# Three mantissa bits of float64 weights taken by ScalarE, and one VectorE operation for each attention tile's bias and threshold

## Chip, cores and metric

The kernel runs on one core of one Trainium2 chip. The metric is the device time of one execution in microseconds. The engines are PE (TensorE, with PEld for its weight loads), DVE (VectorE), ACT (ScalarE), POOL (GpSimd) and SP (SyncE, which here issues nearly all transfers).

## What is computed

Three layers in a row on 2304 tokens of width 512. The second layer's weights arrive as float64.

```python
scores = scale * np.matmul(q, k.transpose(0, 1, 3, 2))        # 4 batches, 8 heads, 576 x 576, depth 64
thresh = np.max(scores, axis=-1, keepdims=True) - tau
scores = np.where(scores >= thresh, scores, -1000000000.0)
scores = scores - np.max(scores, axis=-1, keepdims=True)
attn = np.exp(scores)
attn = attn / (np.sum(attn, axis=-1, keepdims=True) + 1e-09)
x = np.matmul(attn, v)                                        # then heads side by side: 2304 x 512
...
xn = x / rms * rms_g
g = xn @ w_gate                                               # 512 x 1536
x = (g * sigmoid(g) * (xn @ w_val)) @ w_out                   # 1536 x 512
...
P = 8 rounds of row and column scaling of exp(x @ w_gate)     # 8 experts
out += P[:, e:e + 1] * (np.maximum(x @ w1[e], 0.0) @ w2[e])   # for each expert e
```

## The kernel before

**Number format.** Matrices are split into a high and a low f16 part, and a product is three f16 matmuls. The float64 weights of the second layer are read as pairs of 32-bit words. `to_f32` makes a float32 of each: ACT turns the upper word, read as a float, into the right exponent (L441, `wo<-wgatew`, the name `wo` is the staging place). DVE shifts the lower word right by 29, which leaves its top three bits (L442, into `lw`, shown as `wgatel`, `wvall` or `wol`). DVE shifts the float left by three and ORs those bits in (L444). DVE puts the sign in (L445). Each such piece is 128 rows of 512 weights. There are 36: 12 of `w_gate`, 12 of `w_val`, 12 of `w_out`. ACT then squares each piece (L465 for gate and val, whose column sums PE takes; L499 for `w_out`), scales come from that, and L474 and L475 write the high and low parts of `wg` and `wv`. L516 to L518 write those of `wo` when all 12 pieces of `w_out` are done, a maximum over all partitions (`womx`) is known, and the scale is made.

**Attention.** There are 144 tiles of 128 query rows by 576 keys: 36 in each batch, one for each head and block of rows (`att_tile`). PE makes the scores `S` (L282) in one of two PSUM buffers. DVE takes the maximum of each row (L296, into column 2 of the small tile `nt`). ACT multiplies it with a factor `wt` to give the bias of the exponential (L297, column 0), and adds `bt` to it to give the threshold (L301, column 1). ACT makes `e = exp(c2 * S + bias)` (L300), and DVE zeroes what lies under the threshold, and sums the rows (L302). Only L302 frees the buffer of `S`. ACT and POOL then split `e` into `hl` (L307 to L309), SP turns it by a DMA transpose into `eT` (L319), and four tiles later PE multiplies it with `v` (L339, `pv`).

**Order of the work.** Attention of batch 0 runs beside the preparation of the weights. When 16 tiles have gone through `end_main` and `finish_x` (L355 to L362), the second layer starts on PE: `mlp_in` (12 groups `gv` of 24 matmuls, L539, emptied by ACT L547 and DVE L548 and L549) and `mlp_out` (72 matmuls, L573). From there on attention tiles and the second layer share all engines until about 620 us. The third layer (L1020 and L1088) follows to the end. A scheduler works out the order on each engine from dependences and a cost of each instruction, with attention ahead of all else, so a changed instruction can reorder its neighbours. Each engine then executes its list strictly in that order.

Of the kernel before, what the change touches and what calls it, by code (L numbers as in the profile page):

```python
# [8 lines left out]
F16 = mybir.dt.float16  # L9
BF16 = mybir.dt.bfloat16  # L10
I32 = mybir.dt.int32
AF = mybir.ActivationFunctionType
ALU = mybir.AluOpType
AX = mybir.AxisListType
# [5 lines left out]
def kernel(  # L20
# [29 lines left out]
    P = 128  # L50
# [6 lines left out]
    NW = NCH + 1  # L57
# [3 lines left out]
    def small(shape, name, dt=F32, bufs=1):  # L61
        return p0.tile(shape, dt, tag=name, name=name, bufs=bufs)
# [130 lines left out]
    def prep_q_scales(st):  # L193

        b, qr = st["b"], st["raw_q"]
        s_k, i_k = st["k"]
        qm = small([P, NW], "qm", bufs=2)
        for c in range(NW):
            sq = pa.tile([P, H, 2, D], F16, tag="ks", name=f"qq{b}_{c}", bufs=2)
            A.activation(  # L200
                sq[:, :, 0, :].bitcast(BF16), qr[:, :, c, :], AF.Square, accum_out=qm[:, c : c + 1]
            )
        s_q, i_q = norm_scale(qm, NW, 9, f"q{b}")

        wt = small([P, NW], f"wt_{b}")
        bt = small([P, NW], f"bt_{b}")
        V.tensor_scalar(bt, s_q, s_k[:, 0:1], ntau8[:, 0:1], ALU.mult, ALU.mult)
        c2 = small([P, NW], f"c2_{b}")
        V.tensor_scalar(c2, i_q, i_k[:, 0:1], z8[:, 0:1], ALU.mult, ALU.mult)
        V.tensor_scalar(wt, i_q, i_k[:, 0:1], nz8[:, 0:1], ALU.mult, ALU.mult)  # L210
        st.update(wt=wt, bt=bt, c2=c2, s_q=s_q)

    def prep_k(st, a):
# [57 lines left out]
    def att_tile(st, c, heads, slot, group):  # L271

        kT = st["kT"]
        qT, qX = st["q", c]
        nm = f"{st['b']}_{c}_{heads[0]}"
        sums = group["sums"]
        sp = psa.tile([P, 2, 512], F32, tag="S", name=f"S{nm}", bufs=2)
        rows = P // len(heads)
        for qq, first in ((qT, True), (qX, False)):
            for i, h in enumerate(heads):  # L280
                for j in range(2):
                    last = T.matmul(  # L282
                        sp[i * rows : (i + 1) * rows, j, 0:HS],
                        lhsT=qq[:, h, 0:rows],
                        rhs=kT[h // H2][:, h % H2, j * HS : (j + 1) * HS],
                        start=first,
                        stop=not first,
                    )
        if len(waiting) == LAG:
            with tc.issue_after(last.ins):  # L290
                att_values(*waiting.pop(0))
        turn()
        sv = sp[:, :, 0:HS]
        nt = pa.tile([P, 3], F32, tag="nt", name=f"nt{nm}", bufs=4)
        mx = nt[:, 2:3]
        V.tensor_reduce(mx, sv, AX.XY, ALU.max)  # L296
        A.activation(nt[:, 0:1], mx, AF.Copy, scale=st["wt"][:, c : c + 1])  # L297
        e = pa.tile([P, S], F32, tag="e", name=f"e{nm}", bufs=3)
        ev = e.rearrange("p (a n) -> p a n", a=2)
        A.activation(ev, sv, AF.Exp, bias=nt[:, 0:1], scale=st["c2"][:, c : c + 1])  # L300
        A.activation(nt[:, 1:2], mx, AF.Identity, bias=st["bt"][:, c : c + 1])  # L301
        V.scalar_tensor_tensor(  # L302
            ev, sv, nt[:, 1:2], ev, ALU.is_ge, ALU.mult, accum_out=sums[:, slot : slot + 1]
        )

        hl = pa.tile([P, 2 * S], F16, tag="hl", name=f"hl{nm}", bufs=3)
        A.activation(hl[:, 0:S], e, AF.Copy)  # L307
        G.tensor_tensor(hl[:, S + REM :], e[:, 0 : NCH * P], hl[:, 0 : NCH * P], ALU.subtract)  # L308
        G.tensor_tensor(hl[:, S : S + REM], e[:, NCH * P :], hl[:, NCH * P : S], ALU.subtract)  # L309
        waiting.append((st, heads, slot, group, nm))  # L310
        split[nm] = hl
# [110 lines left out]
    def words(src, name, tag="tT"):  # L422

        if tag == "tT":
            r = pw.tile([P, 4, 2, 2 * P], F16, tag=tag, name=name, bufs=4)
            r = r.rearrange("p f l n -> p (f l n)").bitcast(I32)
        else:
            r = pw.tile([P, 4, HD], F32, tag=tag, name=name)
            r = r.rearrange("p o d -> p (o d)").bitcast(I32)
        nc.sync.dma_start(out=r, in_=src)  # L430
        return r.rearrange("p (n w) -> p n w", w=2)

    def to_f32(dst, word, name):

        lw = pw.tile([P, 2, 2, HD], F16, tag="xs", name=name, bufs=2)
        lw = lw.rearrange("p o l n -> p (o l n)").bitcast(I32)  # L440
        A.activation(dst, word[:, :, 1].bitcast(F32), AF.Copy, scale=2.0**-112)  # L441
        V.tensor_scalar(lw, word[:, :, 0], 29, None, ALU.logical_shift_right)  # L442
        di = dst.bitcast(I32)
        V.scalar_tensor_tensor(lw, di, 3, lw, ALU.logical_shift_left, ALU.bitwise_or)  # L444
        V.scalar_tensor_tensor(  # L445
            di, word[:, :, 1], -(2**31), lw, ALU.bitwise_and, ALU.bitwise_or
        )
        return lw
# [785 lines left out]
```

## Time and profile before

| | us |
|---|---|
| median of 3 runs (all: 2121.09, 2122.43, 2131.33) | 2122.43 |
| profiled execution | 2124.11 |
| its span between first and last instruction | 2122.3 |
| PE busy (share of the span) | 1951.8 (92%) |
| DVE busy | 1628.7 (77%) |
| ACT busy | 1307.6 (62%) |
| POOL busy | 1357.4 (64%) |

The profile cuts the span into 40 slices of 53 us. PE is busy for one to four tenths of the first three, and for eight or nine tenths of nearly all others. DVE is at nine tenths in the second and third slice. A busy time is the union of an engine's instructions. An instruction's duration is longer than the time until the next one may start (its step), because neighbours overlap a little. So costs of an engine that has no pause are read as the distance of two starts.

### The profile page before, as it was taken

The page shows a single profiled execution, that of the slowest core. Times are in us where ns is not written, and L with a number is a line of the kernel's source. Part 1 is how long each engine was busy: PE and PEld are TensorE (multiplying, and loading weights), DVE is VectorE, ACT ScalarE, POOL GpSimd, SP SyncE. Part 2 cuts the span into 40 slices and gives each one's busy share as a digit, 9 for nine tenths or more (in the row PEclk, how much of TensorE's full clock was granted, in tenths as well). Part 3 has the DMA queues.
Part 4 walks back from the last instruction along what each step waited for, and adds up shares of the span by engine and source line. Part 5 has one row for each costly group of instructions (what it writes and reads, how often), then busy time and mean ns, then how long its engine had stood idle before and what let it go on. Part 6 is the DMA issues. An engine that isn't in the chain of part 4 may idle for free.

```text
span 2122.3 us, 43825 instructions
## 1 busy us (share of the span) xinstructions
PE 1951.8 (92%) x16462; PEld 1453.5 (68%) x16462; DVE 1628.7 (77%) x3408; ACT 1307.6 (62%) x2804; POOL 1357.4 (64%) x1412
## 2 busy tenths in 40 slices
PE   1348889998999899899999999999999999999998
PEld 0227667667777667677777777777777777777777
DVE  6999777777753445897888888888888878888865
ACT  6888787877753356556655555565555555555552
POOL 0347556656753456667777767777677777777754
PEclk9959999999999999999999999999999999999999
DMA  9986778878756736333433443444334334443332
GB/s 260 224 191 126 158 145 163 169 132 142 134 96 147 186 104 183 123 109 121 140 121 122 125 144 118 124 124 135 120 114 142 118 124 121 141 125 120 102 100 80
DMA packets 373094, 290.47 MB, mean 137 GB/s; under 512 B 286160, under 2 KB 299344, under 8 KB 372880
## 3 DMA queue, kind: packets, MB, share of 16 engines
q1 hardware_dynamic: 371712, 285.81, 52.3%
q8 instruction: 129, 2.11, 0.4%
q0 software_dynamic: 640, 1.84, 0.3%
q14 instruction: 85, 0.70, 0.1%
q10 hardware_dynamic: 528, 0.02, 0.0%
HBM read 195.71 MB, written 21.23 MB: 102 GB/s over the span
## 4 chain that ended last, share of the span: by engine, by line
PE 67%; DVE 2%; SPq 1%; DMA 1%; POOL 1%; ACT 0%; issue 0%; DVEq 0%; POOLq 0%; ACTq 0%
PE P L1088 31%; PE X L1020 17%; PE Z L1020 13%; PE gv L539 3%; PE x L573 2%; SPq L831 1%; DVE w L731 1%; DMA w1r<-in_moe_w_dram 0%; DMA xo<-x2d 0%; DMA eT<-hl 0%; DVE acc L1102 0%; PE logits L873 0%; PE pv L339 0%; DVE w1mx L133 0%; DVE h L999 0%
## 5 line engine op out<-in xcount | busy, mean ns | idle before, releaser
L1088 PE MATMUL P<-w,h 128*128 128x256 f16 x6048 | 769.8, 273 | 12.3 <-DVE w1mx L133 7.6
L1088 PEld LDWEIGHTS <-h 128*128 128x128 f16 x6048 | 592.4, 98 | 151.6 <-issue 15.6
L1020 PEld LDWEIGHTS <-w 128*128 128x128 f16 x4032 | 394.8, 98 | 194.1 <-issue 2.9
L1098 DVE SCALAR_TENSOR_TENSOR acc<-P,coef,acc 128x256 f32<-128x256 f32 x882 | 413.2, 477 | 101.3 <-PE P L1088 90.4
L1020 PE MATMUL X<-xo,w 128*128 128x384 f16 x2304 | 437.9, 327 | 1.3 <-ACT u2b L1040 0.9
L1020 PE MATMUL Z<-xo,w 128*128 128x384 f16 x1728 | 327.9, 326 | 0.0
L308 POOL TENSOR_TENSOR hl<-e,hl 128x512 f16<-128x512 f32 x144 | 174.1, 1209 | 226.9 <-ACT hl L307 148.1
L539 PE MATMUL gv<-xnT,wg 128*128 128x256 f16 x1296 | 170.5, 282 | 17.4 <-DVE u L549 11.9
L539 PE MATMUL gv<-xnT,wv 128*128 128x256 f16 x1296 | 168.5, 276 | 0.0
L539 PEld LDWEIGHTS <-wg 128*128 128x128 f16 x1296 | 128.3, 101 | 38.6 <-issue 18.4
L573 PE MATMUL x<-wo,tT 128*128 128x512 f16 x648 | 143.8, 379 | 3.8 <-DVE u L549 2.5
L539 PEld LDWEIGHTS <-wv 128*128 128x128 f16 x1296 | 126.4, 99 | 16.6 <-issue 0.2
L302 DVE SCALAR_TENSOR_TENSOR e<-S,nt,e 128x576 f32<-128x576 f32 x144 | 116.6, 810 | 24.8 <-ACT e L300 24.4
L296 DVE TENSOR_REDUCE nt<-S 128x1 f32<-128x576 f32 x144 | 107.0, 750 | 26.7 <-PE S L282 25.9
L300 ACT ACTIVATE e<-S,nt,c 128x576 f32<-128x576 f32 x144 | 117.8, 818 | 0.0
L282 PE MATMUL S<-kT,qT 128*128 128x288 f16 (+1 forms) x320 | 65.2, 311 | 56.4 <-DVE e L302 52.1
L573 PEld LDWEIGHTS <-tT 128*128 128x128 f16 x648 | 62.4, 98 | 75.2 <-ACT wo L517 2.7
L339 PEld LDWEIGHTS <-eT 128*128 128x128 f16 (+1 forms) x2240 | 89.1, 106 | 33.4 <-DMA eT<-hl 18.5
L307 ACT ACTIVATE hl<-e 128x576 f16<-128x576 f32 x144 | 97.0, 675 | 23.9 <-DVE e L302 14.8
L339 PE MATMUL pv<-vs,eT 128*128 128x64 f16 (+1 forms) x2240 | 97.4, 201 | 14.8 <-DMA eT<-hl 12.5
L554 POOL TENSOR_TENSOR tT<-u,tT 128x256 f16<-128x256 f32 x108 | 75.4, 699 | 54.7 <-ACT tT L553 54.3
L548 DVE SCALAR_TENSOR_TENSOR u<-u,gv 128x256 f32<-128x256 f32 x108 | 44.8, 415 | 63.7 <-ACT u L547 61.8
(2540 smaller groups left out, 3675.8 us busy)
## 6 DMA issues: line engine op xcount, KB each, us to landing
xo<-x2s SPq DMA_DIRECT2D x319, 384.0 KB, 3.1
w1r<-in_moe_w_dram SPq DMA_DIRECT2D x17, 1024.0 KB, 5.1
w2r<-in_moe_w_dram SPq DMA_DIRECT2D x17, 1024.0 KB, 6.7
x2s<-xo SPq DMA_DIRECT2D x17, 384.0 KB, 3.6
wgatew<-in_moe_w_gate_dram SPq DMA_DIRECT2D x12, 512.0 KB, 6.0
wo<-in_moe_w_out_dram SPq DMA_DIRECT2D x12, 512.0 KB, 4.3
wvalw<-in_moe_w_val_dram SPq DMA_DIRECT2D x12, 512.0 KB, 4.5
qX<-qT SPq DMA_DIRECT2D x40, 128.0 KB, 2.7
```

What stands on the lines that cost most here:

```text
L296: V.tensor_reduce(mx, sv, AX.XY, ALU.max)
L300: A.activation(ev, sv, AF.Exp, bias=nt[:, 0:1], scale=st["c2"][:, c : c + 1])
L302: V.scalar_tensor_tensor(ev, sv, nt[:, 1:2], ev, ALU.is_ge, ALU.mult, accum_out=sums[:, slot : slot + 1])
L307: A.activation(hl[:, 0:S], e, AF.Copy)
L308: G.tensor_tensor(hl[:, S + REM :], e[:, 0 : NCH * P], hl[:, 0 : NCH * P], ALU.subtract)
L339: T.matmul(o, lhsT=a, rhs=r, start=n == 0, stop=n == len(mm) - 1)
L539: T.matmul(gv[:, a, :], lhsT=w[:, l, kk, f * P : (f + 1) * P], rhs=xt[:, r * KD + kk, :], start=n == 0, stop=n == 3 * KD - 1,)
L554: G.tensor_tensor(t[:, 1, :], u, t[:, 0, :], ALU.subtract)
L573: T.matmul(ps, lhsT=tT[f][:, l, o : o + P], rhs=wo[:, f, r, :], start=n == 0, stop=n == 3 * KF - 1,)
L1020: T.matmul(ps, lhsT=w[:, a, l, kk, f * P : (f + 1) * P], rhs=xb[:, r * 2 + kk, :], start=n == 0 and j in (0, 1, 3), stop=n == 5, skip_grou ...
L1088: T.matmul(ps, lhsT=hs[u, ao, f][:, l, jj * P : (jj + 1) * P], rhs=w2[h][:, bo, r, f, :], start=n == 0 and j in (0, 1, 3), stop=n == 5, sk ...
L1098: main[True] = V.scalar_tensor_tensor(y, ps, coef[h][:, i : i + 1], y, ALU.mult, ALU.add)
```

## The change

Two edits. In `to_f32` the shift on DVE is gone. ACT reads the upper 16 bits of the lower word as an unsigned integer, multiplies by 2^-13, subtracts a half (but for 2^-15) and writes an integer, whose rounding gives the top three bits. In `att_tile` the two ACT operations are gone. `wt` and `bt` become pairs, (factor, 1) and (0, offset), and one DVE operation makes both columns of `nt` from the row maximum. The pairs take two buffers in turn for four batches, and each batch adds two small memsets.

```diff
-        wt = small([P, NW], f"wt_{b}")
-        bt = small([P, NW], f"bt_{b}")
-        V.tensor_scalar(bt, s_q, s_k[:, 0:1], ntau8[:, 0:1], ALU.mult, ALU.mult)
+        wt = small([P, NW, 2], "wt", bufs=2)
+        bt = small([P, NW, 2], "bt", bufs=2)
+        V.memset(wt[:, :, 1], 1.0)
+        V.memset(bt[:, :, 0], 0.0)
+        V.tensor_scalar(bt[:, :, 1], s_q, s_k[:, 0:1], ntau8[:, 0:1], ALU.mult, ALU.mult)
...
-        V.tensor_scalar(wt, i_q, i_k[:, 0:1], nz8[:, 0:1], ALU.mult, ALU.mult)
+        V.tensor_scalar(wt[:, :, 0], i_q, i_k[:, 0:1], nz8[:, 0:1], ALU.mult, ALU.mult)
...
-        A.activation(nt[:, 0:1], mx, AF.Copy, scale=st["wt"][:, c : c + 1])
+        V.scalar_tensor_tensor(nt[:, 0:2], st["wt"][:, c], mx, st["bt"][:, c], ALU.mult, ALU.add)
         e = pa.tile([P, S], F32, tag="e", name=f"e{nm}", bufs=3)
         ev = e.rearrange("p (a n) -> p a n", a=2)
         A.activation(ev, sv, AF.Exp, bias=nt[:, 0:1], scale=st["c2"][:, c : c + 1])
-        A.activation(nt[:, 1:2], mx, AF.Identity, bias=st["bt"][:, c : c + 1])
...
-        return r.rearrange("p (n w) -> p n w", w=2)
+        return r.rearrange("p (n w) -> p n w", w=2), r.bitcast(U16).rearrange("p (n w) -> p n w", w=4)
...
-    def to_f32(dst, word, name):
+    def to_f32(dst, words, name):
+        word, half = words
...
-        V.tensor_scalar(lw, word[:, :, 0], 29, None, ALU.logical_shift_right)
+        A.activation(lw, half[:, :, 1], AF.Copy, scale=2.0**-13, bias=2.0**-15 - 0.5)
```

The lines after the edits move down by four at most. In the changed kernel the conversion is L445 (upper word) and L446 (new) on ACT and L448 and L449 on DVE. The attention tile is L299 (maximum), L300 (new, on DVE), L303 (exponential) and L304 (threshold and sum).

On ACT, at the first pieces of `w_gate`, before:

```order
L441 ACTIVATE wo<-wgatew_0_877 128x512
L441 ACTIVATE wo<-wgatew_1_887 128x512
L255 ACTIVATE qs_0_160<-raw_q_112,q_s 128x8x64
L224 ACTIVATE ks_0_0_169<-raw_k_104,k_s 128x4x64 x2
L465 ACTIVATE wgateq_0_884<-wo 128x512
```

Now:

```order
L445 ACTIVATE wo<-wgatew_0_859 128x512
L446 ACTIVATE wgatel_0_861<-wgatew_0_859 128x512
L258 ACTIVATE qs_0_162<-raw_q_112,q_s 128x8x64
L227 ACTIVATE ks_0_0_171<-raw_k_104,k_s 128x4x64 x2
L445 ACTIVATE wo<-wgatew_1_869 128x512
L446 ACTIVATE wgatel_1_871<-wgatew_1_869 128x512
```

ACT now has two whole-piece operations for every piece ahead of DVE's two.

On DVE, where the first group of the second layer (`gv_0`) is emptied (`u_0`), before:

```order
L445 SCALAR_TENSOR_TENSOR wo<-wo_1709,wol_1711 128x512
L296 TENSOR_REDUCE nt_3_1_2115<-S_3_1_2094 128x1
L302 SCALAR_TENSOR_TENSOR e_3_0_2066,sums_3_2041<-S_3_0_2042,nt_3_0_2063,e_3_0_2066 128x576
L501 TENSOR_TENSOR om<-om,igv 128x12
L548 SCALAR_TENSOR_TENSOR u_0_1270<-u_0_1270,gv_0_1245 128x256
L501 TENSOR_TENSOR om<-om,igv 128x12
L549 SCALAR_TENSOR_TENSOR u_0_1270<-u_0_1270,gv_0_1245 128x256
```

Now:

```order
L449 SCALAR_TENSOR_TENSOR wo<-wo_1651,wol_1653 128x512
L552 SCALAR_TENSOR_TENSOR u_0_1252<-u_0_1252,gv_0_1227 128x256
L304 SCALAR_TENSOR_TENSOR e_3_0_2044,sums_3_2019<-S_3_0_2020,nt_3_0_2041,e_3_0_2044 128x576
L299 TENSOR_REDUCE nt_3_1_2092<-S_3_1_2071 128x1
L553 SCALAR_TENSOR_TENSOR u_0_1252<-u_0_1252,gv_0_1227 128x256
L300 SCALAR_TENSOR_TENSOR nt_3_1_2092<-wt,nt_3_1_2092,bt 128x2
L299 TENSOR_REDUCE nt_3_2_2135<-S_3_2_2114 128x1
L552 SCALAR_TENSOR_TENSOR u_1_1284<-u_1_1284,gv_1_1259 128x256
L300 SCALAR_TENSOR_TENSOR nt_3_2_2135<-wt,nt_3_2_2135,bt 128x2
L304 SCALAR_TENSOR_TENSOR e_3_1_2095,sums_3_2019<-S_3_1_2071,nt_3_1_2092,e_3_1_2095 128x576
L553 SCALAR_TENSOR_TENSOR u_1_1284<-u_1_1284,gv_1_1259 128x256
L448 SCALAR_TENSOR_TENSOR wol_1661<-wo,wol_1661 128x512
```

Before, the last of the 36 pieces is done ahead of `u_0` (L501 takes the maxima of `w_out` right behind it). Now 31 are done there, and five pieces of `w_out` stand among the groups of the second layer.

On DVE, two tiles of batch 1 (blocks 2, heads 0 and 1), before:

```order
L296 TENSOR_REDUCE nt_2_0_3756<-S_2_0_3735 128x1
L302 SCALAR_TENSOR_TENSOR e_1_7_3726,sums_1_3411<-S_1_7_3702,nt_1_7_3723,e_1_7_3726 128x576
L345 TENSOR_SCALAR rsum_3890<-sums_1_3411 128x8
L346 RECIPROCAL rsum_3890<-rsum_3890 128x8
L302 SCALAR_TENSOR_TENSOR e_2_0_3759,sums_2_3734<-S_2_0_3735,nt_2_0_3756,e_2_0_3759 128x576
L296 TENSOR_REDUCE nt_2_1_3788<-S_2_1_3767 128x1
```

Now:

```order
L299 TENSOR_REDUCE nt_2_0_3708<-S_2_0_3687 128x1
L347 TENSOR_SCALAR rsum_3838<-sums_1_3371 128x8
L300 SCALAR_TENSOR_TENSOR nt_2_0_3708<-wt,nt_2_0_3708,bt 128x2
L348 RECIPROCAL rsum_3838<-rsum_3838 128x8
L552 SCALAR_TENSOR_TENSOR u_10_2885<-u_10_2885,gv_10_2860 128x256
L299 TENSOR_REDUCE nt_2_1_3739<-S_2_1_3718 128x1
L553 SCALAR_TENSOR_TENSOR u_10_2885<-u_10_2885,gv_10_2860 128x256
L304 SCALAR_TENSOR_TENSOR e_2_0_3711,sums_2_3686<-S_2_0_3687,nt_2_0_3708,e_2_0_3711 128x576
L300 SCALAR_TENSOR_TENSOR nt_2_1_3739<-wt,nt_2_1_3739,bt 128x2
L304 SCALAR_TENSOR_TENSOR e_2_1_3742,sums_2_3686<-S_2_1_3718,nt_2_1_3739,e_2_1_3742 128x576
```

The new L300 rarely stands right behind its maximum. Another operation lies between in 133 of the 144 tiles, and in 19 of them it is (or includes) another tile's L304, as for `nt_2_1` here.

## Rows read from the trace of the kernel before

**Rows 1.** Busy us (x instructions) of each engine in three stretches (windows view).

```profile
core 0: us, PE busy (x) PEld busy (x) DVE busy (x) ACT busy (x) POOL busy (x), PEclk, DMA share, GB/s
25.00:161.00 136.00, 54.54 (x400) 31.30 (x400) 128.37 (x273) 110.08 (x225) 42.41 (x45) 0.81 0.89 213
161.00:237.00 76.00, 67.86 (x696) 49.70 (x697) 67.81 (x157) 58.30 (x135) 48.72 (x59) 0.95 0.64 126
237.00:620.00 383.00, 354.91 (x3960) 270.78 (x3958) 285.58 (x683) 302.80 (x700) 237.48 (x328) 0.98 0.78 146
```

**Rows 2.** PE's waits, 25 to 161 us: us in total, times, longest.

```profile
PE S L282 <- DVE e L302: 39.6, 12, 7.0
PE wvaln L466 <- ACT wvalq L465: 15.5, 7, 6.1
```

**Rows 3.** PE's waits from 237 to 620 us (waits view).

```profile
PE S L282 <- DVE e L302: 10.1, 6, 3.2
PE pv L339 <- DMA eT<-hl: 8.7, 14, 2.1
PE gv L539 <- ACT x2f L593: 4.0, 3, 2.5
PE gv L539 <- DVE u L549: 2.9, 4, 1.2
PE x L573 <- ACT nt L297: 1.3, 1, 1.3
```

**Rows 4.** DVE at a weight piece: start us, duration us (timeline).

```profile
26.81 0.42 DVE L442 TENSOR_SCALAR wgatel<-wgatew 128x512 int32<-128x512 int32 x1
27.14 0.68 DVE L445 SCALAR_TENSOR_TENSOR wo<-wgatew,wgatel 128x512 int32<-128x512 int32 x1
27.75 0.68 DVE L444 SCALAR_TENSOR_TENSOR wgatel<-wo,wgatel 128x512 int32<-128x512 int32 x1
```

**Rows 5.** ACT, two tiles' small operations and a piece's conversion (timeline).

```profile
45.00 0.28 ACT L297 ACTIVATE nt<-nt,wt 128x1 f32<-128x1 f32 x1
45.19 0.28 ACT L301 ACTIVATE nt<-nt,bt 128x1 f32<-128x1 f32 x1
45.37 0.65 ACT L441 ACTIVATE wo<-wgatew 128x512 f32<-128x512 f32 x1
45.93 0.28 ACT L297 ACTIVATE nt<-nt,wt 128x1 f32<-128x1 f32 x1
```

**Rows 6.** ACT's squares of `w_out` pieces, 25 to 161 us: busy us, mean ns.

```profile
L499 ACT ACTIVATE wol<-wo 128x512 bf16<-128x512 f32 x9 | 5.6, 622 | 0.4 <-DVE wo L445 0.4
```

**Rows 7.** DVE, a four-column operation with a scalar from SBUF (timeline).

```profile
37.80 0.22 DVE L471 TENSOR_SCALAR wgategs<-g_sb,wgate_s 128x4 f32<-128x4 f32 x1
37.94 0.14 DVE L485 TENSOR_SCALAR g<-wgate_i 128x1 f32<-128x1 f32 x1
```

**Rows 8.** DVE and POOL meeting at one moment (timeline).

```profile
416.15 1.15 POOL L308 TENSOR_TENSOR hl<-e,hl 128x512 f16<-128x512 f32 x1
...
416.29 1.56 DVE L362 SCALAR_TENSOR_TENSOR xn<-x,rs,xn 128x512 f16<-128x512 f32 x1 [0.30 <-ACT xn L361]
...
417.26 0.76 POOL L309 TENSOR_TENSOR hl<-e,hl 128x64 f16<-128x64 f32 x1
```

**Rows 9.** All L362 on whole tiles: duration ns min/median/max (source view).

```profile
L362 DVE SCALAR_TENSOR_TENSOR xn<-x,rs,xn x16: 734/820/1603, 117.7 to 619.0; 128x512 f16<-128x512 f32 x16
```

**Rows 10.** One attention tile from its maximum to its threshold (timeline).

```profile
173.41 0.75 DVE L296 TENSOR_REDUCE nt<-S 128x1 f32<-128x576 f32 x1
...
174.08 0.41 DVE L548 SCALAR_TENSOR_TENSOR u<-u,gv 128x256 f32<-128x256 f32 x1
174.20 0.29 ACT L297 ACTIVATE nt<-nt,wt 128x1 f32<-128x1 f32 x1
...
174.58 0.82 ACT L300 ACTIVATE e<-S,nt,c 128x576 f32<-128x576 f32 x1
...
175.44 0.82 DVE L302 SCALAR_TENSOR_TENSOR e<-S,nt,e 128x576 f32<-128x576 f32 x1 [0.49 <-ACT e L300]
```

More of the change, by code (lines that the diff above doesn't have):

```diff
@@ L11 @@
 I32 = mybir.dt.int32
+U16 = mybir.dt.uint16
 AF = mybir.ActivationFunctionType
```

## The prediction

> **What bounds the kernel now.** I read first the busy times by stretch, then what PE waits for in each, then single operations. The windows view [rows 1] shows three stretches that the change touches. From 25 to 161 us DVE is busy for 128.4 of 136 us while PE has work for 54.5. This is the prologue: weights are prepared beside the attention of batch 0, and DVE is the bound. PE's own waits say the same [rows 2]: 39.6 us for the operation that frees a score buffer, and 15.5 us for ACT's squares, which stand behind DVE's conversion. From 161 to 237 us, the first pass of the second layer, PE and DVE are both at 89% (67.9 and 67.8 of 76). From 237 to 620 us PE is the bound, 354.9 of 383. The 28 us that it loses go mostly to short waits [rows 3]: 10.1 us in 6 waits for score buffers, 8.7 in 14 for the transposed probabilities, 4.0 in 3 for ACT's copy of the layer's output. Behind 620 us nothing is edited, and from there on the order of the rows on all engines is that of before. PE runs through in the third layer, so I carry what is won or lost by 620 us to the end unchanged.
>
> **Prices of the operations.** The shift on DVE takes 0.33 us from its start to the next (26.81 to 27.14), and the two operations behind it in a piece 0.61 each [rows 4]. ACT's two small operations take 0.19 each, and ACT's conversion of a piece 0.56 (45.37 to 45.93) [rows 5]. The new ACT operation also reads 512 spaced elements and writes 512, so I price it like that conversion, 0.56. Below it could be some hundredths less; above I take twice that, since no row shows 16-bit input. The new DVE operation has two columns and a scalar from SBUF. The nearest row is the four-column one, 0.14 from start to start [rows 7].
>
> To that comes a wait which the small tile doesn't show. L362 reads two tensors from SBUF, as the new operation does (`wt` and `bt`), while the big operations of an attention tile read the scores from PSUM. At 416.29 us an L362 starts 0.14 us behind a POOL operation and lasts 1.56 us, until 0.55 us behind POOL's end, and the next small POOL operation then takes 0.76 us [rows 8]. Over 16 of them the shortest is 0.73 and the longest 1.60 us [rows 9]. So such an operation stands still until POOL is through. The mean of that wait is the chance to meet POOL, times half of a POOL operation [rows 1]: 42.4/136 = 0.31 times half of 42.4/45 = 0.94, 0.15 us, in the prologue; 0.64 times 0.41 = 0.26 in the first pass; 0.62 times 0.36 = 0.22 later. The Trainium skill has this as a rule (SBUF — State Buffer, Who interferes with whom): a DVE instruction with two SBUF inputs contends with a GpSimd instruction that reads SBUF, and whichever is second blocks for the whole of the other. The trace agrees in the row at 416.29; by that rule the new operation is a contender, which the two ACT operations were not.
>
> **Prologue, 25 to 161 us.** PE's first `gv` stands behind the scores of the 24th tile, so I count what each engine has to do ahead of that tile's threshold. DVE loses 35 shifts, 35 x 0.33 = 11.6 us. The schedule also moves five pieces of `w_out` behind this point, 10 x 0.61 = 6.1. It gains 24 new operations, 24 x (0.14 + 0.15) = 7.0. Together -10.7 us. ACT gains 30 conversions, 30 x 0.56 = 16.8, loses 48 small operations, 9.1, and moves five conversions (2.8) and four squares (4 x 0.62 = 2.5 [rows 6]) to later: +2.4 us, to 112.5. If DVE keeps its 7.6 us of idle time, the first `gv` comes 10.7 us earlier. Then ACT would be at 90%, and each piece now goes through ACT twice before DVE can begin and once after. Transfers (0.89 busy) would be near 0.9 too, with five fewer loads. If those two hold the pace, nothing is won. I take -7, between -11 and 0.
>
> **First pass, 161 to 237 us.** The five pieces come back: +6.1 us on DVE, less one shift (0.3), and 12 new operations cost 12 x (0.14 + 0.26) = 4.8. That is +10.6 us on an engine with 8.2 us idle. ACT gets six new operations (3.4) and the moved 5.3 and loses 24 small ones (4.6), +4.1 us with 17.7 idle. The `w_out` parts are needed by `mlp_out` at the end of this stretch, so the delay can't slip further. At best the idle time takes 8.2 of it and 2.4 remain; at worst all 10.6. PE has work here anyhow, which favours the lower half: +4.
>
> **Second layer, 237 to 620 us.** 108 new operations put 108 x (0.14 + 0.22) = 38.9 us on DVE, to 324.5 of 383 (85%). ACT is relieved of 216 x 0.19 = 41.0 us, to 261.8 (68%). Neither is the bound. What counts is the way from a tile's maximum to its exponential. Before, the maximum ends at 174.16 (173.41 + 0.75), and the exponential starts at 174.58: 0.42 us, the two ACT operations [rows 10]. Now, where an operation of some 0.7 us lies between (a maximum 0.75, a `u` 0.41 or a threshold 0.82 [rows 10]), it is 0.7 + 0.14 + 0.22 + 0.04 = 1.1 us. Queued behind the new operation when POOL holds it are all of DVE's emptying of `gv` and the next thresholds, and ACT's exponential waits for it. If all 20 waits for buffers and transposes grow by 0.68 us, that is +13.6. If none grows, and ACT's relief takes away its own two (4.0 + 1.3 [rows 3]), it is -5.3. Four tiles of lag between scores and `pv` cover most of such delays, so I take +1.
>
> **Sum.** -7 + 4 + 1 = -2 us. The profiled execution took 2124.1 us (span 2122.3 and 1.8 around it), so it would come to 2122.1. It lies 1.7 us above the median of 2122.43, on which I put the forecast: 2120.4 us, no difference that can be measured. About 0.5% (10.6 us, below 2111.8 or above 2133.0) is what a measurement of this kernel can tell from no change.
>
> **Rivals.** *The prologue's gain lasts.* DVE at 94% speaks for it; the pieces that only move to the next stretch speak against. It takes -10.7, only 2.4 given back, and -5.3 from ACT's relief: -13.6, 2108.8 us. It decides if the first `gv` starts before about 151 us. *DVE's new operations become the bound (slower).* The place is the way from maximum to exponential from 161 us on, the mechanism the wait for POOL and the operation put between. For it speak POOL's 62% [rows 1] and the 1.6 us of L362; against it that DVE has a quarter of its time free. It keeps -7 in the prologue, loses all 10.6 in the first pass and 13.6 later: +17.2, 2139.6 us. It decides from a mean of about 0.4 us for the new operation, and a longer wait for score buffers than the 10.1 us. By the skill's rule named above this is where the time would go, since each of the 144 operations can be blocked for a whole GpSimd instruction. *The conversion is dearer than it looks.* If ACT needs 1.1 us for 16-bit input, the prologue's ACT work rises by 30 x 0.56 = 16.8 to 129 of 136 us, the gain of 7 is gone, and +4 + 1 give 2127 us. The change then doesn't do what it says, as DVE's work is only exchanged for ACT's.
>
> **How the numbers follow.** Chances: forecast 0.5, lasting gain 0.2, DVE the bound 0.2, dear conversion 0.1. The range runs from the lasting gain's 2109 to 2138, just under the slow rival; beyond each end lies about half of that rival, 0.2 together. The forecast's own range is 2112 to 2133. Faster by over 0.5% has 0.2, slower by over 0.5% has 0.2, within 0.5% has 0.6 (forecast and dear conversion).
>
> **What would show it.** Right, if the profile of the changed kernel shows: the new ACT operation at 0.65 us like L441; the first `gv` at 152 to 156 instead of at 161 us, the border of the first stretch; DVE's five moved pieces between the first groups, and the first pass of `mlp_out` ending 0 to 6 us earlier than before; the new DVE operation at about 0.2 us alone and up to 1.3 beside POOL; ACT's busy time from 237 to 620 us lower by some 40 and DVE's higher by about as much, with PE's waits there near 28 us. Wrong, if the score-buffer waits of that stretch exceed 20 us, if the first `gv` doesn't move, or if a difference appears behind 620 us.

## The result, and the profile after

The changed kernel takes 2137.51 us (median of 6 runs, 2132.87 to 2141.66), the kernel before 2121.76 us over 6 runs. The ratio is 1.0062, with a 95% interval from 1.0043 to 1.0080. So the change makes the kernel slower by 0.62%, some 13 us (the two medians lie 15.8 us apart, within the interval). The forecast was no measurable difference, 2120.4 us. The time lies just inside the stated range, but on the side that had a chance of 0.2.

The profiled execution took 2141.02 us (span 2139.2). Compared with before, PE is idle for 184.3 us instead of 170.5 (+13.8), and busy for 1954.9 us instead of 1951.8 (+3.1). Together that is the 16.9 us by which the span grew. The matmuls are the same 16462 in both, at a mean granted clock of 0.967 instead of 0.978. The windows view of the changed kernel, in the stretches of [rows 1]:

```profile
core 0: us, PE busy (x) PEld busy (x) DVE busy (x) ACT busy (x) POOL busy (x), PEclk, DMA share, GB/s
25.00:161.00 136.00, 61.83 (x485) 37.01 (x484) 123.65 (x268) 115.51 (x205) 46.92 (x50) 0.64 0.86 209
161.00:237.00 76.00, 59.49 (x575) 41.83 (x575) 64.60 (x157) 53.39 (x110) 42.98 (x51) 0.95 0.59 117
237.00:620.00 383.00, 344.92 (x3737) 261.62 (x3738) 302.76 (x750) 253.44 (x468) 226.47 (x308) 0.97 0.74 143
```

PE does more in the prologue (61.83 us instead of 54.54), less in the first pass (59.49 instead of 67.86), and less in the second layer (344.92 instead of 354.91). So idle time changes by -7.3, +8.4 and +10.0 us (most of the rest lies between 620 and 1000 us). Busy time is not quite the same as work, as the granted clock of the prologue differs (0.81 and 0.64). So the matmuls are counted too: 485 instead of 400 in the prologue, 575 instead of 696 in the first pass, 3737 instead of 3960 in the second layer. If the start of the n-th matmul is taken in both traces, the changed kernel is 8.5 us ahead where the kernel before stands at 161 us, 4.5 us behind at 237, 7.8 behind at 260 and 16.8 behind at 640. (The order of the matmuls differs until then, so the values between are rough.) At 237 us both have done 288 matmuls of `gv` and 72 of `mlp_out`. What is missing is attention's: 8 of the scores and 29 of `pv`. In the first pass no engine is as busy as before: DVE fell from 67.81 to 64.60, ACT from 58.30 to 53.39. Whatever is slow there is not an engine with too much work. PE's waits from 237 to 620 us (us in total, times, longest), to be held against [rows 3]:

```profile
PE S L285 <- DVE e L304: 16.9, 12, 4.7
PE gv L543 <- DVE u L553: 10.2, 10, 3.0
PE pv L341 <- DMA eT<-hl: 9.3, 8, 2.1
PE gv L543 <- ACT x2f L597: 3.5, 1, 3.5
```

The waits for DVE have grown: for score buffers from 10.1 to 16.9, for the groups' `u` from 2.9 to 10.2 us. Those for transfers (8.7 and 9.3 us) and for ACT (5.3 and 3.5 us) have not.

The two new operations cost what was expected. The conversion on ACT (source view: ns min/median/max), and the new DVE operation (groups from 25 to 161, 161 to 237 and 237 to 620 us: busy us, mean ns):

```profile
L446 ACT ACTIVATE wgatel<-wgatew x12: 645/652/683, 21.2 to 90.7; 128x512 int32<-128x512 uint16 x12
```

```profile
L300 DVE SCALAR_TENSOR_TENSOR nt<-wt,nt,bt 128x2 f32<-128x2 f32 x25 | 6.5, 261 | 0.0
...
L300 DVE SCALAR_TENSOR_TENSOR nt<-wt,nt,bt 128x2 f32<-128x2 f32 x13 | 4.5, 362 | 0.0
...
L300 DVE SCALAR_TENSOR_TENSOR nt<-wt,nt,bt 128x2 f32<-128x2 f32 x98 | 40.4, 424 | 0.3
```

So the question is not what the operations take. It is where 16.9 us of span come from.

### The profile page after: what moved, and what is told of

Same layout as the page of the kernel before. It is cut to its first block, busy times and chain, and to the rows that moved or that the text cites. A ratio compares the mean times of both kernels' runs of the same rounds, so it can differ in the third digit from the quotient of the medians.

```text
span 2139.2 us, 43709 instructions
## 1 busy us (share of the span) xinstructions
PE 1954.9 (91%) x16462; PEld 1453.0 (68%) x16462; DVE 1661.8 (78%) x3524; ACT 1274.3 (60%) x2552; POOL 1360.0 (64%) x1412
## 3 DMA queue, kind: packets, MB, share of 16 engines
q1 hardware_dynamic: 371712, 285.81, 51.3%
## 4 chain that ended last, share of the span: by engine, by line
PE 72%; DVE 12%; DMA 6%; ACT 4%; issue 3%; POOL 2%; SPq 1%; ACTq 0%; DVEq 0%; POOLq 0%
PE P L1092 30%; PE X L1024 17%; PE Z L1024 12%; PE gv L543 6%; PE x L577 5%; DVE e L304 2%; DVE nt L299 2%; DMA kT<-ks 1%; PE S L285 1%; DMA eT<-hl 1%; DVE nt L300 1%; DMA qT<-qs 1%; PE pv L341 1%; ACT e L303 1%; DVE wo L449 1%
## 5 line engine op out<-in xcount | busy, mean ns | idle before, releaser
L303 ACT ACTIVATE e<-S,nt,c 128x576 f32<-128x576 f32 x144 | 116.9, 824 | 66.2 <-DVE nt L300 51.5
L304 DVE SCALAR_TENSOR_TENSOR e<-S,nt,e 128x576 f32<-128x576 f32 x144 | 115.6, 811 | 32.8 <-ACT e L303 31.7
L543 PEld LDWEIGHTS <-wv 128*128 128x128 f16 x1296 | 127.6, 100 | 17.2 <-issue 0.2
L299 DVE TENSOR_REDUCE nt<-S 128x1 f32<-128x576 f32 x144 | 106.2, 749 | 23.6 <-PE S L285 22.8
L285 PEld LDWEIGHTS <-qT 128*128 128x128 f16 (+1 forms) x320 | 23.2, 102 | 105.5 <-DVE e L304 81.0
```

What stands on the lines that cost most here:

```text
L285: last = T.matmul(sp[i * rows : (i + 1) * rows, j, 0:HS], lhsT=qq[:, h, 0:rows], rhs=kT[h // H2][:, h % H2, j * HS : (j + 1) * HS], start= ...
L304: V.scalar_tensor_tensor(ev, sv, nt[:, 1:2], ev, ALU.is_ge, ALU.mult, accum_out=sums[:, slot : slot + 1])
L543: T.matmul(gv[:, a, :], lhsT=w[:, l, kk, f * P : (f + 1) * P], rhs=xt[:, r * KD + kk, :], start=n == 0, stop=n == 3 * KD - 1,)
```

## Experiments

Each time is stated as the ratio to the kernel before on the same chip. 0.1% is 2.1 us.

### One edit alone

`conv_only` has the edit of `to_f32` and the attention tile of before. `att_only` has the attention tile of the changed kernel and this line of before:

```diff
-        A.activation(lw, half[:, :, 1], AF.Copy, scale=2.0**-13, bias=2.0**-15 - 0.5)
+        V.tensor_scalar(lw, word[:, :, 0], 29, None, ALU.logical_shift_right)
```

> The kernel before with the conversion edit alone: ScalarE makes the low bits, the attention tile keeps its two ScalarE operations. All 36 pieces stay ahead of the first group here, so nothing moves into the first pass. Theory (the loss comes from the new VectorE operation standing still beside GpSimd, and from the five moved pieces): VectorE loses 36 shifts of 0.33 us, ScalarE gains 36 operations of 0.56 and becomes the nearer limit; the first gv comes 3 to 8 us earlier than 161 us, first pass and second layer take what they took before (70 and 383 us); 2112 to 2120 us. Rival (the conversion itself is what costs, as an exchange of VectorE's work for ScalarE's): first gv at 161 us or later, 2125 to 2140 us.

> The attention edit alone; the shift stays on VectorE, and all 36 pieces stay ahead of the first group. Theory (blocked operation): the 100 or so new operations behind the first group last 0.42 us in the mean, up to over 1 us; from the end of the first pass to the end of attention the kernel falls behind by some 10 to 15 us, as in the changed kernel, the prologue loses 2 to 6 us by 24 operations more on VectorE, the first pass loses nothing to moved pieces: 2132 to 2142 us. Rival (the loss of the changed kernel hangs on the moved pieces, and later tiles merely inherit it): 2120 to 2128 us.

`conv_only` 0.9984 [0.9974, 0.9994] (2121.32 us); `att_only` 1.0028 [1.0015, 1.0041] (2129.69). Both medians lie between the ranges of theory and rival. One edit wins 0.16%, the other loses 0.28%. Together they should lose 0.12%, and they lose 0.62%. Half a per cent belongs to neither edit alone. One thing that occurs only with both: alone, each edit leaves all 36 pieces ahead of the first group, as before. Together, the schedule puts five pieces of `w_out` behind it.

### The operation without its second SBUF input

`psum_max` is the changed kernel, `psum_att_only` the attention edit alone, with the maximum written beside the scores in PSUM:

```diff
-        mx = nt[:, 2:3]
+        mx = sp[:, 0, HS : HS + 1]
...
-        V.scalar_tensor_tensor(nt[:, 0:2], st["wt"][:, c], mx, st["bt"][:, c], ALU.mult, ALU.add)
+        V.scalar_tensor_tensor(
+            nt, mx.to_broadcast([P, 2]), st["bt"][:, c : c + 1], st["wt"][:, c], ALU.add, ALU.mult
+        )
```

> The changed kernel, but the row maximum is written beside the scores in their own PSUM buffer, and the new operation reads it from there, so that it has one tensor input from SBUF instead of two: nt = (maximum + offset) x (factor, 1). The exponential is thereby scaled by a constant that the division by the row sums takes out again. Count and place of VectorE's operations stay, the five or six pieces stay moved. Theory (two SBUF inputs make it wait for GpSimd): the new operation lasts 0.2 to 0.25 us, none above 0.5; behind the first pass the loss of 12 us shrinks to 0 to 4, the first pass keeps its loss of 14, the prologue its gain of 9: 2123 to 2130 us. Rival (what costs is one more operation in VectorE's line between maximum and exponential, however long it is): 2134 to 2142 us, as the changed kernel.

> As the kernel with the attention edit alone, with the maximum in PSUM as in psum_max; the shift stays on VectorE, all pieces ahead of the first group. Theory (two SBUF inputs): against att_only the second layer gets back 8 to 12 us; 2118 to 2128 us. Rival (one more operation in line): within 3 us of att_only.

`psum_max` 1.0049 [1.0034, 1.0064] (2134.11 us); `psum_att_only` 1.0092 [1.0077, 1.0107] (2143.59). The first lies in the range of the rival, the second is slower than either range. In both the operation never lasts over 0.22 us, so the stall beside POOL is gone (groups from 25 to 660 us in `att_only`, then in `psum_att_only`):

```profile
L300 DVE SCALAR_TENSOR_TENSOR nt<-wt,nt,bt 128x2 f32<-128x2 f32 x144 | 54.2, 384 | 0.6
```

```profile
L299 DVE SCALAR_TENSOR_TENSOR nt<-S,bt,wt 128x2 f32<-128x2 f32 x144 | 28.7, 211 | 0.3
```

Half of the operation's time is saved, and yet the one kernel gains at most little (0.13%, and the intervals overlap), while the other loses. My theory of the stall falls as the main cause. (The schedule of `psum_max` puts six pieces behind the first group instead of five, so it is not the same order.) Why `psum_att_only` is 14 us slower than `att_only` stays open. The order of ACT's and DVE's rows is the same in both through the prologue, but in the profiled executions the first weight piece reaches DVE at 21.78 instead of 19.48 us, and the twelfth threshold comes 5 us later. Behind the prologue the orders differ, and there most of the loss arises: by the n-th matmul it is 4.4 us at 161 us and 16.5 at 640.

### What waits for the moved pieces

The trace of the changed kernel shows a hole in attention that no theory so far has named. Between 199.39 and 231.21 us no tile's maximum is taken. The two rows on DVE (start us, duration us):

```profile
199.39 0.75 DVE L299 TENSOR_REDUCE nt<-S 128x1 f32<-128x576 f32 x1
231.21 1.41 DVE L299 TENSOR_REDUCE nt<-S 128x1 f32<-128x576 f32 x2
```

It is the change from batch 0 to batch 1. The keys of batch 1 need their scale, which needs a maximum over all partitions, made by a matmul (`kmxp`) whose input `kmm` is an operation of DVE:

```profile
91.53 0.15 DVE L181 TENSOR_REDUCE kmm<-km 128x1 f32<-128x3 f32 x1
```

```profile
198.29 0.22 PE L132 MATMUL womxp<-ident,om 128*128 128x128 bf16 x1
199.69 0.22 PE L132 MATMUL kmxp<-ident,kmm 128*128 128x128 bf16 x1
```

`kmm` is there at 91.53 us, and the matmul runs at 199.69, right behind that of `w_out`'s maximum (`womxp`). All such maxima share one PSUM buffer (`tag="mx", ... bufs=1`) in the order of the code, and `w_out`'s comes first. So the last weight piece holds up the next batch's attention. Before, it is the same pair of rows, with a hole of 26.6 us from 203.5 us on:

```profile
186.81 0.22 PE L131 MATMUL womxp<-ident,om 128*128 128x128 bf16 x1
189.11 0.22 PE L131 MATMUL kmxp<-ident,kmm 128*128 128x128 bf16 x1
```

So the change makes the hole longer by 5.2 us; it was there before. With `conv_only`, `womxp` runs at 174.65, and no hole between 161 and 260 us is over 9 us.

To test this, `after_keys_early`, `before_keys_early` and `conv_keys_early` take batch 1's keys and values ahead of it, in the changed kernel, in the kernel before and in `conv_only`:

```diff
-        if o == (4 if early else 20):
+        if o == (4 if early else 14):
...
-        if o == (10 if early else 23):
+        if o == (10 if early else 17):
...
-        if o == (12 if early else 24):
+        if o == (12 if early else 18):
```

`att_double` is the changed kernel with the new operation twice in each tile (`for _ in range(2):`). Its schedule keeps all 36 pieces ahead of the first group.

> The changed kernel, but batch 1's keys and values are loaded at tile 14 and their scales made at tiles 17 and 18 instead of 20, 23 and 24, so that their maximum over partitions takes the one PSUM buffer mx ahead of the maximum of w_out (womx). The pieces stay moved behind the first groups. Theory (womx gates batch 1: in the changed kernel the matmul of kmx stands until 199.7 us behind womx at 198.3, though its input is there at 91.5, and attention has no new tile from 199.4 to 231.2 us): the gap closes, PE loses 6 to 12 us less between 200 and 260 us; 2124 to 2132 us. Rival (the loss comes from the new VectorE operation in the second layer): the first pass changes, the end doesn't, 2134 to 2142 us.

> The kernel before with the same edit of batch 1's keys. There the gap is from 203.5 to 230 us, behind womx at 187. Theory (womx gates batch 1): it closes here too, and PE loses 3 to 7 us less between 200 and 260 us; 2114 to 2120 us. Rival (before had enough other matmuls in the gap): 2120 to 2126 us.

> The conversion edit alone with the same edit of batch 1's keys. With the conversion alone womx ended at 175 us, and attention had no gap over 7 us. Theory (womx gates batch 1): little is left to win, 0 to 4 us: 2116 to 2122 us. Rival (any earlier key helps by as much as it helps the changed kernel): 2108 to 2115 us.

> The changed kernel with the new VectorE operation twice in each tile, so that the price of that operation is doubled. The schedule then keeps all 36 pieces ahead of the first group and womx behind 24 thresholds instead of 35. Theory (moved pieces and womx make the loss; the operation itself costs about 6 us, as the attention edit alone): twice 6 and no late womx, 2128 to 2138 us, not slower than the changed kernel. Rival (the loss is the operation's): 2 x 16, 2145 to 2160 us.

`after_keys_early` 1.0042 [1.0027, 1.0057] (2134.68 us); `before_keys_early` 0.9987 [0.9977, 0.9998] (2122.07); `conv_keys_early` 0.9939 [0.9921, 0.9957] (2111.97); `att_double` 1.0051 [1.0035, 1.0068] (2136.86). `kmxp` now runs at 87 to 99 us, and the hole is gone. But `after_keys_early` gains only 0.2% on the changed kernel, less than expected and not clear of noise. Its pieces and `womxp` come still later (205.95 us), and the first pass of `mlp_out` ends at 255 us instead of 233. `conv_keys_early` gains 0.45% on `conv_only`, where the theory had seen little left to win. That is the time that its rival gave, and the fastest kernel of the study, 0.61% faster than before. `before_keys_early` gains 0.13%, as its rival had it. `att_double` decides the other question: twice the operation, with no piece moved, is no slower than the changed kernel.

### The pieces moved, and moved back

`before_pieces_behind` and `conv_pieces_behind` tie the last five pieces behind the groups 0 to 4, with neither edit and with the conversion alone:

```diff
-            sq = to_f32(wo32[:, f], wd, f"wol{f}").bitcast(BF16)[:, 0:DM]
+            if f < KF - 5:
+                lw = to_f32(wo32[:, f], wd, f"wol{f}")
+            else:
+                with tc.issue_after(ends[f - KF + 5].ins):
+                    lw = to_f32(wo32[:, f], wd, f"wol{f}")
+            sq = lw.bitcast(BF16)[:, 0:DM]
```

`ends` holds the last DVE operation of each group. `after_keys_pieces` is `after_keys_early` with the pieces at attention's priority, `after_pieces_ahead` the changed kernel with the first `u` tied behind all pieces (`prep_pieces` is the loop over `f` of `prep_out`, `made[0]` the last piece's operation):

```diff
+                with attention_order():
+                    prep_pieces()
                 tT = mlp_in(0)
                 prep_out()
```

```diff
+            with tc.issue_after(made[0].ins):
+                V.scalar_tensor_tensor(u, u, 1.0, gv[:, 0, :], ALU.add, ALU.mult)
```

> The kernel before with neither edit: only the last five pieces of w_out are tied behind the groups 0 to 4 of the second layer on VectorE, as they stand in the changed kernel (31 pieces ahead of the first u, womx behind 36 thresholds and 9 groups). Theory (the moved pieces make most of the loss): PE starts the first gv a few us earlier than 161 us, loses 8 to 14 us between 200 and 260 us, and the kernel takes 2130 to 2138 us. Rival (the loss is the new VectorE operation's, and the moved pieces are a side show): within 4 us of before, 2120 to 2126 us.

> The conversion edit alone, with the last five pieces of w_out tied behind the groups 0 to 4 in the same way. Theory (moved pieces): 8 to 14 us slower than the conversion edit alone (2121 us), 2127 to 2136 us. Rival (new VectorE operation): 2118 to 2124 us.

> The changed kernel with batch 1's keys early, and the pieces of w_out traced at attention's priority, so that 33 instead of 30 stand ahead of the first u and womx stands behind 29 thresholds instead of 35. Theory (moved pieces): against the changed kernel with early keys (2134.7 us) 6 to 14 us are won back, 2120 to 2129 us; what is left above the conversion edit with early keys (2112 us) is the price of the new operation in the second layer. Rival (the new operation costs 16 to 22 us beside the conversion in whatever order): 2130 to 2138 us.

> The changed kernel with all 36 pieces tied ahead of the first u on VectorE. The first u then stands behind 32 thresholds instead of 24, so that some of the early start is lost. Theory (moved pieces): 3 to 12 us faster than the changed kernel, 2126 to 2134 us. Rival (new operation): 2135 to 2142 us.

`before_pieces_behind` 1.0013 [1.0004, 1.0023] (2126.53 us); `conv_pieces_behind` 1.0029 [1.0020, 1.0039] (2130.24); `after_keys_pieces` 0.9979 [0.9969, 0.9988] (2120.27); `after_pieces_ahead` 1.0054 [1.0039, 1.0069] (2135.00).

The theory held in the second and third of these, and missed in the other two. Moving the pieces behind costs the conversion kernel 0.45% (0.9984 to 1.0029, 9.6 us). Moving three of six pieces forward (33 instead of 30 ahead of the first `u`, `womxp` at 183.32 us instead of 205.95) wins 0.63% (1.0042 to 0.9979, 13 us) where the keys are early. In the kernel before the move behind costs 0.13%, though `womxp` then runs at 203.16 us and the hole lasts 35.6 us, longer than in the changed kernel. So neither the late maximum nor the hole sets the price by itself. It seems to depend on what else is late; on what exactly, these runs don't tell. In `after_pieces_ahead` the move forward wins nothing that can be told from zero. There the first `u` stands behind 32 thresholds instead of 24, so that the pieces come forward by holding up the groups, and `womxp` comes only 3 us earlier (195.22 us).

### What is left of the attention edit

`keys_pieces_psum` is `after_keys_pieces` with the maximum in PSUM, by the edit of `psum_max`. In the traces the rows of ACT, DVE and POOL stand in the same order (but for the memsets of `bt`), and one matmul of PE has moved. `thr_on_dve` and `bias_on_dve` start from the kernel before and move only one of its two small operations to DVE:

```diff
-        A.activation(nt[:, 1:2], mx, AF.Identity, bias=st["bt"][:, c : c + 1])
+        V.scalar_tensor_tensor(nt[:, 1:2], mx, 1.0, st["bt"][:, c : c + 1], ALU.mult, ALU.add)
```

```diff
-        A.activation(nt[:, 0:1], mx, AF.Copy, scale=st["wt"][:, c : c + 1])
+        V.scalar_tensor_tensor(nt[:, 0:1], mx, 1.0, st["wt"][:, c : c + 1], ALU.mult, ALU.mult)
```

> The changed kernel with early keys and the pieces at attention's priority (2120 us, 0.9979 of before), and with the maximum in PSUM, so that the new operation doesn't wait for GpSimd. The counts of pieces, thresholds and groups in VectorE's order are those of that kernel. Standing still beside GpSimd costs the 0.3 to 0.4%: 4 to 8 us faster, 2112 to 2116 us (0.994 to 0.996). The place in line costs it: 2117 to 2124 us (0.997 to 1.000).

> The kernel before (no conversion edit), with only the threshold's operation moved to VectorE, as one operation with two tensor inputs from SBUF; the bias stays on ScalarE. So there are 144 operations that stand still beside GpSimd, but none between maximum and exponential. Place in line: within 3 us of before, 2120 to 2127 us. Standing still: 4 to 8 us slower, as the attention edit alone, 2127 to 2133 us.

> The kernel before, with only the bias's operation moved to VectorE, with two tensor inputs from SBUF, between the maximum and the exponential; the threshold stays on ScalarE. Place in line, or standing still: 4 to 10 us slower than before, 2127 to 2135 us; with the threshold's run it tells which. If it is within 3 us of before, neither is the cause, and ScalarE's lost work or the schedule is.

`keys_pieces_psum` 0.9968 [0.9955, 0.9981] (2116.51 us); `thr_on_dve` 1.0053 [1.0032, 1.0075] (2136.01); `bias_on_dve` 1.0044 [1.0027, 1.0062] (2134.47). The first is the clean test of the stall. The groups from 25 to 660 us, `after_keys_pieces` first:

```profile
L300 DVE SCALAR_TENSOR_TENSOR nt<-wt,nt,bt 128x2 f32<-128x2 f32 x144 | 49.3, 350 | 0.5
```

```profile
L299 DVE SCALAR_TENSOR_TENSOR nt<-S,bt,wt 128x2 f32<-128x2 f32 x144 | 29.3, 212 | 0.5
```

DVE is relieved of 20 us, and the ratio falls by 0.0011, or 2.3 us. The intervals overlap, so the stall is worth between nothing and some 6 us of the kernel's time in this order. The other two refute the rival as well. An operation off the way from maximum to exponential costs as much as one on it. In `thr_on_dve` that way, from the end of the maximum to the start of the exponential, is as long as before (from 237 to 620 us a median of 0.84 us, before 0.82). In the changed kernel it is 1.61. PE's busy time in three stretches (one execution each) is:

| | ratio | 25 to 161 us | 161 to 260 us | 260 to 660 us |
|---|---|---|---|---|
| before | 1 | 54.5 | 88.0 | 374.8 |
| changed | 1.0062 | 61.8 | 75.6 | 367.1 |
| `att_only` | 1.0028 | 52.8 | 84.2 | 373.1 |
| `thr_on_dve` | 1.0053 | 53.1 | 81.6 | 373.0 |
| `bias_on_dve` | 1.0044 | 51.3 | 82.5 | 371.2 |
| `conv_pieces_behind` | 1.0029 | 55.8 | 86.0 | 370.2 |
| `after_keys_early` | 1.0042 | 62.0 | 76.2 | 378.5 |
| `after_keys_pieces` | 0.9979 | 61.0 | 84.8 | 374.8 |
| `conv_keys_early` | 0.9939 | 55.7 | 89.6 | 381.0 |

With DVE's operation alone (the three kernels without the conversion), PE does 1 to 3 us less in the prologue, 4 to 6 us less between 161 and 260 us, and 2 to 4 us less later. So the loss falls in no one stretch, though it is densest in the middle one. What makes it, beside the stall, stays open. An operation for both columns (`att_only`) seems to cost less than one for either, but the intervals overlap. Kernels with the same operations in another order lie further apart (`psum_att_only` and `att_only`, 0.64%).

## Why the prediction was wrong, step by step

**Prices: right in size.** The conversion lasts 0.65 us, like L441 [rows 5]. The new operation was put at 0.29 us in the prologue, 0.40 in the first pass and 0.36 later, and its mean duration is 0.26, 0.36 and 0.42. (The prices were distances of two starts, which are shorter than durations, by 0.08 us in [rows 7].) The stall beside POOL has the form that L362 showed [rows 8], from this timeline of the changed kernel, DVE between two operations of POOL:

```profile
92.00 1.30 POOL L310 TENSOR_TENSOR hl<-e,hl 128x512 f16<-128x512 f32 x1 [3.74 <-ACT hl L309]
93.26 0.82 POOL L311 TENSOR_TENSOR hl<-e,hl 128x64 f16<-128x64 f32 x1
```

```profile
92.19 1.12 DVE L300 SCALAR_TENSOR_TENSOR nt<-wt,nt,bt 128x2 f32<-128x2 f32 x1
```

The two columns take until 93.31 us, POOL's end. So the rule of the Trainium skill that the prediction named holds for this tile of two columns too (SBUF — State Buffer, Who interferes with whom). As the prediction read the rule, the time would go into these stalls. It is not where most of it went: the clean test gives 2.3 us.

**Prologue, -7 forecast: right.** The first `gv` starts 8.5 us earlier (before at 161.27 us), inside the stated 152 to 156. PE has 7.3 us less idle time by 161 us.

```profile
152.76 0.83 PE L543 MATMUL gv<-xnT,wg 128*128 128x256 f16 x3
```

**First pass, +4 forecast: the step that failed first.** PE's idle time there grew by 8.4 us, and by 12.4 if the stretch is drawn to 260 us, where the hole ends. By the n-th matmul the loss is 13.0 us by 237 us, above the bound of 10.6. I had seen the five moved pieces, and priced them by DVE's time alone: 10.6 us with the new operations, of which the idle time could take 8.2. I took the lower half since "PE has work here anyhow". DVE's time was not the price: between 161 and 237 us DVE is less busy than before. And PE did not have work enough: at 237 us it is attention's matmuls that are missing. The pieces end a chain: `womx` came at 198.5 instead of 187.1 us, and behind it stand both `mlp_out`'s weights and, through one PSUM buffer, batch 1's keys. A count of work per engine can't show such a tie. The row of `kmxp` would have: in the trace of before it runs at 189.11 us, 102 us behind its input (`kmm`, 87.16). Forcing the five pieces behind cost 0.45%, more than two thirds of the whole, in a kernel without the attention edit. By the n-th matmul, `conv_pieces_behind` is 4.0 us ahead of `conv_only` at 161 us and 4.7 us behind it at 237, and 8.4 behind at 640. So the pieces alone lose 8.7 us in the first pass.

That the pieces' order costs this much is shown for the kernel with the conversion. By which wait it costs it is not: without the hole only 0.2% came back, and in the kernel before the same order cost 0.13%. The sign that I had named for this stretch was no test either. The first pass of `mlp_out` does end earlier, at 232.8 instead of 234.9 us, as forecast. It is attention that fell behind.

**Second layer, +1 forecast: mis-sized.** It came to +10.0 us in the stretch as drawn, within the stated -5.3 to 13.6, but at the other end. I had taken the way from a tile's maximum to its exponential as what counts. It grew by about the 0.68 us of my worst case, by 0.79 in its median and by 0.48 in its mean (1.30 to 1.78 us). The four tiles of lag were to cover it. But `thr_on_dve` doesn't lengthen that way and loses as much, so what counts is something else that the runs don't name. Part of the loss is not the attention edit's: by the numbers above, the pieces alone lose 3.7 us between 237 and 640 us. The attention edit itself, added where the pieces stand alike (31 ahead of the first `u`), costs 0.33% (`conv_pieces_behind` to the changed kernel), or 0.28% alone, 6 to 7 us. Where the keys are early, it is 0.40%, with one more piece behind (`conv_keys_early` to `after_keys_pieces`). Doubled, with the pieces ahead, it costs 0.67% (`conv_only` to `att_double`), twice as much. That ACT is relieved (302.80 to 253.44 us) won little: PE's waits for it were 5.3 us before [rows 3], and are 3.5 now. DVE's busy time grew by 17.2 us there, not by the 40 or so that I had named as a sign. 98 tiles have their maximum in the stretch instead of 106.

**Sum.** -0.16% by the conversion, +0.45% by the moved pieces, +0.33% by the attention edit are 0.62%, as measured. The three are steps from one kernel to the next (before, `conv_only`, `conv_pieces_behind`, changed), so that they add up is no proof. But the middle step changes the order alone, and no operation.

**The rivals.** The slow one, with its 17.2 us and 2139.6 us, is nearly the measured time, and its parts (-7, +10.6, +13.6) nearly those of the trace (-7.3, +8.4 to 12.4, +7.7 to 10.0). Both of its signs came: the new operation's mean reached 0.4 us (0.42), and the score-buffer waits grew from 10.1 to 16.9 us. Yet its mechanism holds in part only, so that much of the hit is luck. The stall is a small share, the operation put between maximum and exponential is no worse than one behind it, and the largest part comes with the pieces' order. The sign by which I would have called the forecast wrong, score-buffer waits over 20 us, was set too high. The dear conversion is out. The lasting gain did exist in the conversion, but not in this kernel: `conv_keys_early` takes 2111.97 us.

**Behind 620 us** the prediction expected no difference. Attention's last threshold now comes at 646.5 instead of 616.5 us, so the shared part is longer than the stretch. By the n-th matmul the lag is 16.8 us at 640 us and hardly changes from there (17.5 at 1000).

## What to carry to other kernels

When a change takes work off a saturated engine, ask which operations the schedule now puts behind others, and follow what waits for the last of them, and not only how long they take. Then test the order by itself, since its price can differ from kernel to kernel (here 0.45% and 0.13%). Look for resources that are single and taken in the order of the code (here one PSUM buffer for all maxima), and for operations that run long after their inputs: they tie together chains that have nothing to do with each other. 144 small operations, some 20 us by the forecast's step of 0.14 us, cost the kernel 6 to 11 us when they came onto an engine that was at 94% and 89% in the first two stretches, and the 49 us of which ACT was relieved in the second layer gave little back.

## What the hardware showed

A stalled operation can miss the gap between two operations of POOL. One L300 lasts 4.43 us, from 567.07 us on, through seven operations of POOL that run back to back (the first and the last of them here):

```profile
567.07 4.43 DVE L300 SCALAR_TENSOR_TENSOR nt<-wt,nt,bt 128x2 f32<-128x2 f32 x1
```

```profile
566.78 0.70 POOL L558 TENSOR_TENSOR tT<-u,tT 128x256 f16<-128x256 f32 x1
...
571.15 0.33 POOL L311 TENSOR_TENSOR hl<-e,hl 128x64 f16<-128x64 f32 x1
```

So the prediction's bound, that the operation stands still until POOL's running one ends, is too low, and so is its sign of up to 1.3 us. But of the 144 it is the only one over 2 us.

The granted clock of the prologue differed more between kernels than PE's work did: 0.81 in its mean before, 0.64 in the changed kernel, 1.00 in `conv_only`, with PE busy for 54.5, 61.8 and 55.8 of 136 us. In the changed kernel it is 1.00 from 40 to 50 us, 0.58 from 50 to 60 and 0.50 (the level of 1.2 GHz) from 60 to 70, after 3.55 and 3.11 us of PE's work in the two 10 us ahead of the fall. `conv_only` had 3.27 and 3.45 us there and stayed at 1.00. Nothing in these rows tells why. That the clock did not decide the time is argued, not tested: PE is idle for more than half of that stretch in all three kernels.
